# Half of the weight chunks joined on VectorE alone, the other half with two-byte instead of one-byte ScalarE stores, and a Newton step of the norms in three VectorE steps

## The chip, the core and the metric

The kernel runs on one core of one Trainium2 chip. The metric is the device time of one execution in microseconds (us). PE is TensorE (matmuls), DVE is VectorE, ACT is ScalarE, POOL is GpSimd, and SP is the queue that issues most DMAs. Each engine works through its own instructions strictly in their order, and waits on the others by semaphores.

## What is computed

Three layers follow one another on 8 batches of 576 tokens with 512 features: a linear attention, a layer that mixes by two Fourier transforms and a two-matrix network (`moe`), and a gated layer (`moe2`), which the change touches only by its weights.

```python
def _moe_ref(x, w_ch1, w_ch2):                      # x: attention output, (8, 576, 512)
    X = np.fft.fft(np.fft.fft(x, axis=1), axis=2)
    u = x + np.real(X)
    mu = np.mean(u, axis=-1, keepdims=True)
    var = np.mean((u - mu) ** 2, axis=-1, keepdims=True)
    un = (u - mu) / np.sqrt(var + 1e-06)
    return u + np.maximum(un @ w_ch1, 0.0) @ w_ch2   # w_ch1 (512, 2048), w_ch2 (2048, 512)
```

All weight matrices are 64-bit floats in memory.

## The kernel before

**Weights.** The two matrices of `moe` come in as 64-bit numbers and are needed as 32-bit floats. They are cut into 32 chunks of 128 x 512 numbers, two chunks to a pair: 16 pairs, numbered 0 to 15 here. A pair is one buffer of 128 x 1024 numbers, each as a low and a high 32-bit word. `assemble` makes 32-bit floats of it in three passes. `low_parts` issues two: DVE shifts the high words left by three (L168, into `wr`), and ACT takes the top three bits of the low words as a small number and stores it as one byte over the lowest byte of the high word (L169). `high_parts` issues the join one step later: DVE combines both (L171). `squares` (L231, ACT) then sums the squares of the pair, `scales` makes a power of two of the sums of a whole matrix, and `split` writes every chunk as two 16-bit halves (ACT L257, DVE L258). Pairs 0 and 1 have buffers of their own (`words`); from pair 2 on four buffers are taken in turn (`u`, `u`, `raw`, `words`), and the load of pair k+4 (L211, SP) waits for the join of pair k. The same `assemble` serves the weights of the last layer in 40 smaller pieces of 128 x 256, beside the main loop.

**The front.** Before the main loop of matmuls can start, the first batch must have passed attention (L311 on) and the transform (`transform`, L448 on: DVE adds, ACT copies, PE matmuls, in turn), the norm of block 0 must be done (`norm_part`, L599 on), the matrices must be joined and the first chunks split. `beside_first` records these strands into each other: for each step of the attention or transform strand 0.4 steps (`RATE`) of the weight strand `front_z`. The final order on every engine is then set at build time by a scheduler from its own estimates of durations; it is fixed when the kernel runs.

**The main loop** (L1076 on) takes 9 blocks of 512 tokens. Per block PE does 16 times `mm1` (L1093) and `mm2` (L1116); attention, transform and norm of later batches and the last layer's weights run beside it as side work. At a block's end the next block's norm must be done: `halves` (ACT L671, DVE L672) makes its 16-bit parts `unh`, `unl`, and L1134 adds the accumulated result to `u`.

**The norm.** After the mean of squares (PE L632) `norm_part` makes 1/sqrt by ACT (logarithm and exponential, L640 and L641, or L649 and L650), refines it by one Newton step on DVE, and multiplies the deviations `d` by it (L658). For blocks 0 and 1 (`i in SUMS_F32`) that step is four DVE instructions, L643 to L646, on 256 columns at a time; for the other seven blocks one (L648) ahead of the logarithm and three (L653 to L655) behind it, on 512 columns.

Of the kernel before, what the change touches and what calls it, by code (L numbers as in the profile page):

```python
# [10 lines left out]
F16 = mybir.dt.float16  # L11
BF16 = mybir.dt.bfloat16
U32 = mybir.dt.uint32
U8 = mybir.dt.uint8
AF = mybir.ActivationFunctionType
ALU = mybir.AluOpType
AX = mybir.AxisListType
# [11 lines left out]
POOL_K = ()  # L29
BEHIND_X = {(1, 1): 6}  # L30
RATE = 0.4
AHEAD_W = 6
FIRST = 1.0
HOLD = {(2, 0): "c"}

MAX_PE = (0, 1, 2)

POOL_N = ()
SUMS_PE = (0,)
SUMS_F32 = (0, 1)  # L40
# [8 lines left out]
def net(ctx, tc, q, k, v, w1, w2, mu_k, mu_r, w_k, w_v, w_r, ce_d, se_d, cs_d, ss_d, alt_d, id_d, out):  # L49
    nc = tc.nc  # L50
# [65 lines left out]
    wsc = big.tile([128, 8], F32, name="wsc")  # L116
# [44 lines left out]
        nc.sync.dma_start(out=raw.rearrange("p n w -> p (n w)"), in_=src.bitcast(U32)[128 * t:128 * t + 128, 512 * c:512 * c + 512])  # L161
        return raw

    def assemble(raw, x, part=None):

        hi, lo = raw[..., 1], raw[..., 0]
        if part != 1:
            nc.vector.tensor_scalar(out=x, in0=hi, scalar1=3, scalar2=0x3FFFFFFF, op0=ALU.logical_shift_left, op1=ALU.bitwise_and)  # L168
            nc.scalar.activation(out=raw.bitcast(U8)[..., 4], in_=lo, func=AF.Copy, scale=0.9975 * 2.0 ** -29, bias=-0.49)  # L169
        if part != 0:  # L170
            nc.vector.scalar_tensor_tensor(out=x, in0=hi, scalar=0xC0000007, in1=x, op0=ALU.bitwise_and, op1=ALU.bitwise_or)  # L171

    def decode(raw, x):

# [3 lines left out]
    pairs = [(w, c) for w in range(2) for c in range(0, 16, 2)]  # L178
    raws = {}
# [33 lines left out]
    def words_at(w, c):  # L213
        a, b = place[w, c] + 1, place[w, c + 1] + 1
        return wr[:, a:b + 1:b - a]

    def low_parts(k):

        if k < len(pairs):
            assemble(raws[k], words_at(*pairs[k]), 0)  # L220

    def high_parts(k):
        if 0 <= k < len(pairs):
            assemble(raws.pop(k), words_at(*pairs[k]), 1)
# [374 lines left out]
    def norm_part(i, sq, d, rs, c0, n):  # L599
        segs = [(b, s + max(c0 - o, 0), min(o + m, c0 + n) - max(o, c0), max(o, c0)) for b, s, m, o in segments(i) if o < c0 + n and o + m > c0]  # L600
        cs = slice(c0, c0 + n)
        tt = nc.vector.tensor_tensor
# [4 lines left out]
        if not onpe:  # L607
# [3 lines left out]
            pt = mean(i, sq, cs, n)  # L611
        else:
            pt = aside(i == 0, 1)
# [9 lines left out]
        if not onpe:  # L623
# [4 lines left out]
            pt = mean(i, sq, cs, n)  # L628
# [9 lines left out]
        w = sq[:, 1, cs]
        if i in SUMS_F32:
            nc.scalar.activation(out=r, in_=pt[:, 0:n], func=AF.Ln, bias=wsc[:, 7:8])  # L640
            nc.scalar.activation(out=r, in_=r, func=AF.Exp, scale=-0.5)  # L641
            yield 1
            tt(out=v, in0=r, in1=r, op=ALU.mult)  # L643
            nc.vector.scalar_tensor_tensor(out=v, in0=pt[:, 0:n], scalar=1e-6, in1=v, op0=ALU.add, op1=ALU.mult)
            nc.vector.tensor_scalar(out=v, in0=v, scalar1=-0.5, scalar2=1.5, op0=ALU.mult, op1=ALU.add)
            tt(out=r, in0=r, in1=v, op=ALU.mult)  # L646
        else:
            nc.vector.tensor_scalar(out=v, in0=pt[:, 0:n], scalar1=1e-6, scalar2=None, op0=ALU.add)  # L648
            nc.scalar.activation(out=r, in_=v, func=AF.Ln)  # L649
            nc.scalar.activation(out=r, in_=r, func=AF.Exp, scale=-0.5)  # L650
            yield 1

            tt(out=w, in0=r, in1=r, op=ALU.mult)  # L653
            nc.vector.scalar_tensor_tensor(out=w, in0=w, scalar=-0.5, in1=v, op0=ALU.mult, op1=ALU.mult)
            nc.vector.scalar_tensor_tensor(out=r, in0=w, scalar=1.5, in1=r, op0=ALU.add, op1=ALU.mult)  # L655
# [730 lines left out]
```

## Time and profile before

| what | value |
|---|---|
| median of 3 runs (lowest to highest) | 1475.55 us (1475.35 to 1476.8) |
| profiled execution, its own time | 1476.24 us |
| its span in the trace | 1474.5 us |
| busy in the span: PE / DVE / ACT | 1407.6 / 989.5 / 705.6 us |
| mean granted clock of TensorE | 0.976 |

The span is what the trace covers; 1.74 us of the profiled execution's own time lie around it. The profiled execution stands 0.69 us above the median.

### The profile page before, as it was taken

Reading aid. Unit: us, or ns where it says so; the run is one execution under the profiler, and the core shown is the slowest. Engines: PE = TensorE matmul, PEld = TensorE weight load, DVE = VectorE, ACT = ScalarE, POOL = GpSimd, SP = SyncE. Lnnn points to the kernel's source line nnn. Section 1 sums busy time; section 2 is a strip of 40 time slices with the busy share of each in tenths; the row PEclk is TensorE's granted clock in tenths of the full one; section 3 lists DMA queues with packets and bytes.
Section 4 is the critical chain, followed back from the end, with each engine's and each line's share of the span. In section 5 each row is a group of like instructions: output and inputs, shape, how many; then the busy total and the mean of one; then the engine's idle time right before and its main releaser. Section 6 shows DMA issues by size and latency. Waiting matters only on the chain.

```text
span 1474.5 us, 20917 instructions
## 1 busy us (share of the span) xinstructions
PE 1407.6 (95%) x8453; PEld 879.7 (60%) x8453; DVE 989.5 (67%) x1807; ACT 705.6 (48%) x1241; POOL 26.5 (2%) x41
## 2 busy tenths in 40 slices
PE   4559999998999999999999999999999999999998
PEld 3447888996555556556455444445666666666665
DVE  6778676587584765764532476774999788876643
ACT  6895643453342443432321246563766555564421
POOL 0101000000000000000000000000000000000000
PEclk8579999999999999999999999999999999999999
DMA  9731012121110111010010023301011011100001
GB/s 349 251 136 51 1 52 80 51 85 45 51 51 29 51 51 63 17 51 30 0 58 7 32 80 117 118 22 58 29 58 51 8 58 58 50 9 29 30 15 43
DMA packets 38301, 89.47 MB, mean 61 GB/s; under 512 B 5147, under 2 KB 11580, under 8 KB 38204
## 3 DMA queue, kind: packets, MB, share of 16 engines
q1 hardware_dynamic: 37052, 85.30, 16.6%
q0 software_dynamic: 1152, 2.83, 0.6%
q8 instruction: 66, 1.08, 0.3%
q14 instruction: 31, 0.25, 0.1%
HBM read 69.25 MB, written 18.87 MB: 60 GB/s over the span
## 4 chain that ended last, share of the span: by engine, by line
PE 88%; DVE 5%; ACT 4%; issue 1%; DMA 1%; ACTq 0%; DVEq 0%
PE h L1093 24%; PE acc L1116 24%; PE acc L1219 13%; PE h L1154 11%; PE side L1207 6%; PE side L509 2%; PE side L529 2%; PE side L430 2%; PE side L375 1%; ACT u L169 1%; PE side L410 1%; DVE wr L258 1%; DVE wr L171 1%; ACT words L169 1%; DMA kt<-in_k_dram 1%
## 5 line engine op out<-in xcount | busy, mean ns | idle before, releaser
L1093 PE MATMUL h<-unh,wr 128*128 128x512 f16 (+1 forms) x1408 | 381.8, 342 | 3.8 <-ACT unh L671 2.0
L1116 PE MATMUL acc<-hh,wr 128*128 128x512 f16 (+1 forms) x1408 | 370.4, 341 | 0.0
L1093 PEld LDWEIGHTS <-wr 128*128 128x128 f16 x2112 | 203.0, 98 | 169.1 <-issue 7.5
L1116 PEld LDWEIGHTS <-wr 128*128 128x128 f16 x2112 | 201.7, 98 | 160.8 <-issue 3.7
L1093 PE MATMUL h<-unl,wr 128*128 128x512 f16 (+1 forms) x704 | 240.6, 342 | 0.7 <-DVE unl L672 0.7
L1116 PE MATMUL acc<-hl,wr 128*128 128x512 f16 (+1 forms) x704 | 220.0, 341 | 0.0
L1219 PE MATMUL acc<-ring,last 128*128 128x512 f16 x864 | 201.2, 379 | 0.2 <-DVE last L1250 0.2
L1099 DVE SCALAR_TENSOR_TENSOR hl<-h,hh 128x512 f16<-128x512 f32 x144 | 99.0, 687 | 145.8 <-ACT hh L1098 145.2
L1098 ACT ACTIVATE hh<-h 128x512 f16<-128x512 f32 x144 | 85.8, 596 | 180.5 <-PE h L1093 179.8
L1219 PEld LDWEIGHTS <-last 128*128 128x128 f16 x864 | 84.0, 98 | 86.5 <-DVE last L1250 0.7
L1154 PEld LDWEIGHTS <-wkh 128*128 128x128 f16 x1008 | 98.5, 98 | 34.1
L1248 ACT ACTIVATE last<-last,pw 128x512 f32<-128x512 f32 x72 | 51.6, 717 | 106.9 <-DVE last L1247 106.3
L1207 PE MATMUL side<-ring,x 128*128 128x512 f16 x432 | 101.1, 379 | 0.0
L1154 PE MATMUL h<-x,wkh 128*128 128x256 f16 x560 | 95.7, 273 | 0.0
L1169 DVE TENSOR_TENSOR last<-h,last 128x512 f32<-128x512 f32 x90 | 61.8, 687 | 49.9 <-PE h L1154 49.8
L1154 PE MATMUL h<-x,wkl 128*128 128x256 f16 x280 | 76.3, 273 | 0.0
L1154 PE MATMUL h<-last,wkh 128*128 128x256 f16 x448 | 76.1, 273 | 0.0
L1207 PEld LDWEIGHTS <-x 128*128 128x128 f16 x432 | 42.3, 98 | 42.5
L1250 DVE TENSOR_TENSOR last<-last 128x512 f16<-128x512 f32 x72 | 49.5, 687 | 22.1 <-ACT last L1249 21.7
L1154 PE MATMUL h<-last,wkl 128*128 128x256 f16 x224 | 61.1, 273 | 0.0
L883 ACT ACTIVATE aa<-y,ms 128x512 f32<-128x512 f32 x72 | 48.0, 712 | 17.5 <-DVE x L891 12.2
L887 DVE SCALAR_TENSOR_TENSOR aa<-y,ms,aa 128x512 f32<-128x512 f32 x72 | 52.4, 747 | 1.2
(350 smaller groups left out, 2074.2 us busy)
## 6 DMA issues: line engine op xcount, KB each, us to landing
vt<-in_v_dram SPq DMA_DIRECT2D x16, 650.0 KB, 5.0
kt<-in_k_dram SPq DMA_DIRECT2D x16, 576.0 KB, 3.9
qt<-in_q_dram SPq DMA_DIRECT2D x16, 576.0 KB, 3.9
out_dram<-oo SPq DMA_DIRECT2D x36, 256.0 KB, 2.0
y<-yT SPq DMA_DIRECT2D x8, 1026.0 KB, 5.3
u<-in_w_dram SPq DMA_DIRECT2D x16, 512.0 KB, 4.5
words<-in_w_dram SPq DMA_DIRECT2D x10, 512.0 KB, 9.8
raw<-in_w_k_dram SPq DMA_DIRECT2D x16, 256.0 KB, 3.7
```

Source lines behind the costliest of these rows:

```text
L883: nc.scalar.activation(out=a, in_=y[:, t, 0:n], func=AF.Copy, scale=mu[:, w, 1, t:t + 1])
L887: nc.vector.scalar_tensor_tensor(out=a, in0=y[:, t, 1:n + 1], scalar=mu[:, w, 0, t:t + 1], in1=a, op0=ALU.mult, op1=ALU.add)
L1093: mm(out=pt[:, o:o + m], lhsT=a, rhs=c[:, t, o:o + m], start=(t == z == 0), stop=(t == 3 and z == 2))
L1098: ma = nc.scalar.activation(out=hh[:, 0:n], in_=pt[:, 0:n], func=AF.Relu)
L1099: mv = nc.vector.scalar_tensor_tensor(out=hl[:, 0:n], in0=pt[:, 0:n], scalar=0.0, in1=hh[:, 0:n], op0=ALU.max, op1=ALU.subtract)
L1116: mm(out=acc[x][:, o:o + m], lhsT=a, rhs=c[:, o:o + m], start=(f == z == o == 0), stop=(f == NF - 1 and z == 2), skip_group_check=(i < 2))
L1154: mm(out=pt[:, 256 * x:256 * x + 256], lhsT=c[:, u, 128 * x:128 * x + 128], rhs=d[:, u], start=(fresh and x == u == z == 0), stop=(last an ...
L1169: nc.vector.tensor_tensor(out=out, in0=view(pt), in1=addend, op=ALU.add)
L1207: mm(out=pt, lhsT=a[:, v, u, c, o:o + 128], rhs=w[:, t, :], start=(t == y == 0), stop=(t == 3 and y == 2))
L1219: mm(out=acc[x], lhsT=a[:, 128 * x:128 * x + 128], rhs=c[:, f, :], start=(f == z == 0), stop=(f == 7 and z == 2))
L1248: nc.scalar.activation(out=o, in_=o, func=AF.Square, scale=W["pw"][:, 10 + g:11 + g])
L1250: nc.vector.tensor_tensor(out=l2, in0=o, in1=h2, op=ALU.subtract)
```

## The change

`assemble` gets a flag `own`, which is set for the pairs with an even number (0, 2, ... 14; `OWN = 0`). For these the ACT store is left out: a second DVE pass (L170 in the changed file) shifts the low words right by 29 and joins them into `wr`, and the join (L174) then adds only the two top bits of the high words. For the odd pairs, and for the 40 pieces of the last layer, ACT still stores, but two bytes in place of one (L172). In the norm the first of the DVE steps of blocks 2 to 8 goes into the logarithm's bias, which blocks 0 and 1 had already; the factor -0.5 moves from the Newton step into the product with `d`, so that three DVE steps (L644 to L646) stay for every block, and the product (L650) becomes a SCALAR_TENSOR_TENSOR.

```diff
-    def assemble(raw, x, part=None):
+    def assemble(raw, x, part=None, own=False):
         hi, lo = raw[..., 1], raw[..., 0]
+        join = nc.vector.scalar_tensor_tensor
         if part != 1:
             nc.vector.tensor_scalar(out=x, in0=hi, scalar1=3, scalar2=0x3FFFFFFF, op0=ALU.logical_shift_left, op1=ALU.bitwise_and)
-            nc.scalar.activation(out=raw.bitcast(U8)[..., 4], in_=lo, func=AF.Copy, scale=0.9975 * 2.0 ** -29, bias=-0.49)
+            if own:
+                join(out=x, in0=lo, scalar=29, in1=x, op0=ALU.logical_shift_right, op1=ALU.bitwise_or)
+            else:
+                nc.scalar.activation(out=raw.bitcast(U16)[..., 2], in_=lo, func=AF.Copy, scale=0.9975 * 2.0 ** -29, bias=-0.49)
         if part != 0:
-            nc.vector.scalar_tensor_tensor(out=x, in0=hi, scalar=0xC0000007, in1=x, op0=ALU.bitwise_and, op1=ALU.bitwise_or)
+            join(out=x, in0=hi, scalar=0xC0000000 if own else 0xC0000007, in1=x, op0=ALU.bitwise_and, op1=ALU.bitwise_or)
...
-            assemble(raws[k], words_at(*pairs[k]), 0)
+            assemble(raws[k], words_at(*pairs[k]), 0, k % 2 == OWN)
...
-            tt(out=v, in0=r, in1=r, op=ALU.mult)
-            nc.vector.scalar_tensor_tensor(out=v, in0=pt[:, 0:n], scalar=1e-6, in1=v, op0=ALU.add, op1=ALU.mult)
-            nc.vector.tensor_scalar(out=v, in0=v, scalar1=-0.5, scalar2=1.5, op0=ALU.mult, op1=ALU.add)
-            tt(out=r, in0=r, in1=v, op=ALU.mult)
-        else:
-            nc.vector.tensor_scalar(out=v, in0=pt[:, 0:n], scalar1=1e-6, scalar2=None, op0=ALU.add)
...
+        tt(out=v, in0=r, in1=r, op=ALU.mult)
+        nc.vector.scalar_tensor_tensor(out=v, in0=pt[:, 0:n], scalar=1e-6, in1=v, op0=ALU.add, op1=ALU.mult)
+        nc.vector.scalar_tensor_tensor(out=r, in0=v, scalar=-3.0, in1=r, op0=ALU.add, op1=ALU.mult)
         yield 0
         for x in range(2):
-            (nc.gpsimd.tensor_tensor if i in POOL_N else tt)(out=d[:, 2 * x:2 * x + 2, cs], in0=d[:, 2 * x:2 * x + 2, cs], in1=r[:, None, :].to_broadcast([128, 2, n]), op=ALU.mult)
+            dx = d[:, 2 * x:2 * x + 2, cs]
+            nc.vector.scalar_tensor_tensor(out=dx, in0=dx, scalar=-0.5, in1=r[:, None, :].to_broadcast([128, 2, n]), op0=ALU.mult, op1=ALU.mult)
```

The changed file is eight lines shorter, so that line numbers behind the norm are eight lower in it, and those in attention and transform three higher. The scheduler's order changes in the whole front. Three places follow.

On ACT, in the front, from the store of pair 4 to the attention of the first batch's second half, before (`qT`, `kt`, `qt`: attention; `wr,amax`: squares):

```order
L169 ACTIVATE raw<-raw 128x1024
L403 ACTIVATE qT<-side_311 128x4x128
L403 ACTIVATE qT<-acc_317 128x4x128
L403 ACTIVATE qT<-acc_329 128x2x64
L231 ACTIVATE wr,amax<-wr 128x1024
L364 ACTIVATE kt<-kt 128x1152
L169 ACTIVATE words<-words 128x1024
L231 ACTIVATE wr,amax<-wr 128x1024 x2
L357 ACTIVATE qt<-qt 128x1152
L169 ACTIVATE u<-u 128x1024
```

The same stretch of ACT with the change:

```order
L234 ACTIVATE wr,amax<-wr 128x1024
L406 ACTIVATE qT<-side_311 128x4x128
L406 ACTIVATE qT<-acc_317 128x4x128
L367 ACTIVATE kt<-kt 128x1152
L406 ACTIVATE qT<-acc_329 128x2x64
L234 ACTIVATE wr,amax<-wr 128x1024
L172 ACTIVATE words<-words 128x1024
L234 ACTIVATE wr,amax<-wr 128x1024 x2
L360 ACTIVATE qt<-qt 128x1152
L388 ACTIVATE kvbd_99<-acc_291,rk 64x64 x4
```

The stores of pairs 4 (`raw`) and 6 (`u`) are gone; that of pair 5 (`words`) stays, and is followed by the same squares and `qt`.

On DVE, a little later in the front, around the joins of pairs 6 and 7 (both `u`), before (`st`, `qt`, `kvbd`: attention; `eo`: transform):

```order
L366 TENSOR_REDUCE st<-qt 128x18
L387 COPY kvbd_99<-kvbd_99 64x2
L171 SCALAR_TENSOR_TENSOR wr<-u,wr 128x2x512
L367 TENSOR_SCALAR st<-st 128x18
L168 TENSOR_SCALAR wr<-u 128x2x512
L368 RECIPROCAL st<-st 128x18
L370 TENSOR_TENSOR qt<-qt,st 128x1152
L464 TENSOR_TENSOR eo<-u 128x288 x2
L171 SCALAR_TENSOR_TENSOR wr<-u,wr 128x2x512
L464 TENSOR_TENSOR eo<-u 128x288 x2
```

The same stretch of DVE with the change:

```order
L170 SCALAR_TENSOR_TENSOR wr<-u,wr 128x2x512
L370 TENSOR_SCALAR st<-st 128x18
L174 SCALAR_TENSOR_TENSOR wr<-u,wr 128x2x512
L371 RECIPROCAL st<-st 128x18
L373 TENSOR_TENSOR qt<-qt,st 128x1152
L467 TENSOR_TENSOR eo<-u 128x288 x2
L168 TENSOR_SCALAR wr<-u 128x2x512
L467 TENSOR_TENSOR eo<-u 128x288 x2
L472 TENSOR_TENSOR x_97<-eo,x_97 1x289
L478 TENSOR_TENSOR eo<-eo 128x289
L174 SCALAR_TENSOR_TENSOR wr<-u,wr 128x2x512
```

Pair 6 now has two DVE passes there (L170, L174) and no ACT store to wait for. The first pass of pair 7 (L168) has moved behind the second half of the attention, so that four instructions of the transform stand between it and its join, where before the end of the attention (L368, L370) stood there too.

On DVE, at the end of the front, from the norm of block 0 to the first `split`, before (`sq`, `rs`, `d`: norm; `m`: attention of the next batch; `wsc<-amax`: scales):

```order
L643 TENSOR_TENSOR rs<-rs 128x256
L336 TENSOR_TENSOR m<-m,kt 64x128
L644 SCALAR_TENSOR_TENSOR rs<-side_581,rs 128x256
L645 TENSOR_SCALAR rs<-rs 128x256
L171 SCALAR_TENSOR_TENSOR wr<-u,wr 128x1024
L646 TENSOR_TENSOR rs<-rs 128x256
L643 TENSOR_TENSOR rs<-rs 128x256
L658 TENSOR_TENSOR d<-d,rs 128x2x256 x2
L644 SCALAR_TENSOR_TENSOR rs<-acc_588,rs 128x256
L240 TENSOR_REDUCE wsc<-amax 128x1
L258 SCALAR_TENSOR_TENSOR wr<-wr,wsc 128x512
```

The same stretch of DVE with the change:

```order
L609 TENSOR_TENSOR sq<-u 128x2x64
L336 TENSOR_TENSOR m<-m,kt 128x256
L339 TENSOR_TENSOR m<-m,kt 64x128 x2
L644 TENSOR_TENSOR rs<-rs 128x256
L645 SCALAR_TENSOR_TENSOR rs<-side_581,rs 128x256
L644 TENSOR_TENSOR rs<-rs 128x256
L646 SCALAR_TENSOR_TENSOR rs<-rs 128x256
L243 TENSOR_REDUCE wsc<-amax 128x1
L645 SCALAR_TENSOR_TENSOR rs<-acc_588,rs 128x256
L650 SCALAR_TENSOR_TENSOR d<-d,rs 128x2x256
L261 SCALAR_TENSOR_TENSOR wr<-wr,wsc 128x512
```

The join of the last pair, 15, has left this stretch: it now stands ahead of it, right behind the subtraction that makes `d` (L621, before L618). One of the two products with `d` comes behind the first split.

## Rows read from the trace of the kernel before

**Rows 1.** Windows: busy time of each engine in stretches, granted clock, DMA

```profile
18.00:109.00 91.00, 47.47 (x203) 39.11 (x201) 66.56 (x117) 81.34 (x117) 4.97 (x8) 0.69 0.62 230
...
160.00:480.00 320.00, 315.63 (x2292) 239.15 (x2290) 211.67 (x370) 132.20 (x254) 7.05 (x8) 0.99 0.15 51
480.00:1022.00 542.00, 542.00 (x2708) 279.60 (x2707) 319.98 (x603) 216.96 (x436) 5.50 (x9) 1.00 0.15 47
1022.00:1474.50 452.50, 448.19 (x2856) 276.51 (x2854) 335.65 (x621) 236.37 (x368) 3.24 (x7) 1.00 0.12 40
```

The columns are: stretch, its length, busy us (and count) of PE, PEld, DVE, ACT and POOL, granted clock, DMA share, GB/s.

**Rows 2.** Waits of DVE from 18 to 109 us: total us, times, longest

```profile
DVE wr L171 <- ACT words L169: 8.5, 5, 3.3
DVE wr L171 <- ACT u L169: 5.5, 5, 1.8
DVE sq L606 <- PE acc L632: 3.2, 1, 3.2
DVE wr L171 <- ACT raw L169: 2.2, 3, 1.3
DVE wr L171 <- ACT seh L137: 2.0, 1, 2.0
DVE wsc L343 <- PE acc L341: 1.3, 1, 1.3
DVE eo L464 <- ACT u L431: 0.5, 1, 0.5
```

**Rows 3.** Line L169, the one-byte stores: ns minimum/median/maximum, first and last start

```profile
L169 ACT ACTIVATE raw<-raw x43: 759/831/2481, 37.8 to 985.3; 128x256 uint8<-128x256 uint32 x40, 128x1024 uint8<-128x1024 uint32 x3
L169 ACT ACTIVATE u<-u x8: 2459/2469/2620, 29.1 to 103.1; 128x1024 uint8<-128x1024 uint32 x8
L169 ACT ACTIVATE words<-words x5: 2457/2471/2533, 18.8 to 88.5; 128x1024 uint8<-128x1024 uint32 x5
```

**Rows 4.** Groups by form, 0 to 160 us: busy us, mean ns, idle before

```profile
L231 ACT ACTIVATE wr<-wr 128x1024 bf16<-128x1024 f32 x16 | 16.9, 1059 | 2.4 <-DVE wr L171 2.2
...
L171 DVE SCALAR_TENSOR_TENSOR wr<-u,wr 128x1024 uint32<-128x1024 uint32 x8 | 9.8, 1223 | 7.5 <-ACT u L169 5.5 <-ACT seh L137 2.0
...
L403 ACT ACTIVATE qT<-side 128x512 f32<-128x512 f32 x6 | 6.9, 1145 | 0.0
...
L168 DVE TENSOR_SCALAR wr<-u 128x1024 uint32<-128x1024 uint32 x8 | 5.4, 678 | 0.0
```

**Rows 5.** Timeline of DVE in the front: start, us, instruction, idle before it

```profile
88.63 0.75 DVE L552 TENSOR_TENSOR u<-u,sd 128x574 f32<-128x574 f32 x1
...
93.11 2.35 DVE L618 TENSOR_TENSOR d<-u,acc 128x1024 f32<-128x1024 f32 x2
...
102.84 0.29 DVE L606 TENSOR_TENSOR sq<-u 128x128 f32<-128x128 f32 x1 [3.23 <-PE acc L632]
...
104.93 0.29 DVE L645 TENSOR_SCALAR rs<-rs 128x256 f32<-128x256 f32 x1
...
109.06 0.75 DVE L258 SCALAR_TENSOR_TENSOR wr<-wr,wsc 128x512 f16<-128x512 f32 x1
```

**Rows 6.** Timeline of PE, the sums of squares of the norm of block 0

```profile
96.88 3.78 PE L632 MATMUL side<-sq,onesr 128*128 128x256 f32 x8 [1.85 <-ACT sq L620]
100.45 2.28 PE L632 MATMUL acc<-sq,onesr 128*128 128x256 f32 x8
```

**Rows 7.** Line L648, the first step of the later norms: ns minimum/median/maximum

```profile
L648 DVE TENSOR_SCALAR rs<-side x7: 692/692/692, 336.5 to 866.8; 128x512 f32<-128x512 f32 x7
```

**Rows 8.** Timeline of PE, the rows with idle time from 345 to 350 us

```profile
346.12 0.59 PE L1093 MATMUL h<-unh,wr 128*128 128x512 f16 x2 [1.96 <-ACT unh L671]
348.84 0.61 PE L430 MATMUL side<-qT,bdh 128*128 128x288 f32 x1 [2.12 <-DVE qTl L405]
```

**Rows 9.** Waits of the SP queue in the whole span: total us, times, longest

```profile
SPq L211 <- DVE wr L171: 40.2, 8, 9.5
```

**Rows 10.** DMA queues from 0 to 110 us

```profile
DMA packets 7680, 27.15 MB, mean 247 GB/s; under 512 B 859, under 2 KB 1020, under 8 KB 7676
```

More of the change, by code (lines that the diff above doesn't have):

```diff
@@ L13 @@
 U32 = mybir.dt.uint32
-U8 = mybir.dt.uint8
+U16 = mybir.dt.uint16
 AF = mybir.ActivationFunctionType
@@ L31 @@
 RATE = 0.4
+OWN = 0
 AHEAD_W = 6
@@ L36 @@
 MAX_PE = (0, 1, 2)
-POOL_N = ()
 SUMS_PE = (0,)
-SUMS_F32 = (0, 1)
 JT = (((0, 128), (128, 128), (225, 64)), ((0, 128), (128, 128), (256, 32)))
@@ L219, in low_parts @@
         if k < len(pairs):
-            assemble(raws[k], words_at(*pairs[k]), 0)
+            assemble(raws[k], words_at(*pairs[k]), 0, k % 2 == OWN)
     def high_parts(k):
         if 0 <= k < len(pairs):
-            assemble(raws.pop(k), words_at(*pairs[k]), 1)
+            assemble(raws.pop(k), words_at(*pairs[k]), 1, k % 2 == OWN)
             if k + 4 >= AHEAD_W:
@@ L637, in norm_part @@
         v, r = rs[:, 0, cs], rs[:, 1, cs]
[L638 to L642, printed above, removed]
-            tt(out=v, in0=r, in1=r, op=ALU.mult)
-            nc.vector.scalar_tensor_tensor(out=v, in0=pt[:, 0:n], scalar=1e-6, in1=v, op0=ALU.add, op1=ALU.mult)
-            nc.vector.tensor_scalar(out=v, in0=v, scalar1=-0.5, scalar2=1.5, op0=ALU.mult, op1=ALU.add)
-            tt(out=r, in0=r, in1=v, op=ALU.mult)
-        else:
-            nc.vector.tensor_scalar(out=v, in0=pt[:, 0:n], scalar1=1e-6, scalar2=None, op0=ALU.add)
[L649 to L655, printed above, removed]
+        nc.scalar.activation(out=r, in_=pt[:, 0:n], func=AF.Ln, bias=wsc[:, 7:8])
+        nc.scalar.activation(out=r, in_=r, func=AF.Exp, scale=-0.5)
+        yield 1
+        tt(out=v, in0=r, in1=r, op=ALU.mult)
+        nc.vector.scalar_tensor_tensor(out=v, in0=pt[:, 0:n], scalar=1e-6, in1=v, op0=ALU.add, op1=ALU.mult)
+        nc.vector.scalar_tensor_tensor(out=r, in0=v, scalar=-3.0, in1=r, op0=ALU.add, op1=ALU.mult)
         yield 0
         for x in range(2):
-            (nc.gpsimd.tensor_tensor if i in POOL_N else tt)(out=d[:, 2 * x:2 * x + 2, cs], in0=d[:, 2 * x:2 * x + 2, cs], in1=r[:, None, :].to_broadcast([128, 2, n]), op=ALU.mult)
+            dx = d[:, 2 * x:2 * x + 2, cs]
+            nc.vector.scalar_tensor_tensor(out=dx, in0=dx, scalar=-0.5, in1=r[:, None, :].to_broadcast([128, 2, n]), op0=ALU.mult, op1=ALU.mult)
             yield 0
```

## The prediction

> **What bounds the kernel now.** I read the windows first. From 160 us to the end PE is busy for all but 4.4 + 0 + 4.3 us of 1314 [rows 1]: there the kernel is PE's own work, which the change leaves alone, and what DVE or ACT save costs and gains nothing. From 18 to 109 us it is different. PE is busy 47.5 of 91 us at a granted clock of 0.69, ACT 81.3 us, DVE 66.6 us [rows 1]. ACT sets the pace of this front, and DVE must be watched, since the change hands it work.
>
> The waits of DVE in these 91 us show how ACT's load reaches the end. DVE is idle 91.0 - 66.6 = 24.4 us, and 8.5 + 5.5 + 2.2 = 16.2 us of it end with a byte store of L169; 2.0 more end with a tiny ACT row (L137) that stands behind such a store, and 1.3 with a PE transpose that waits for an ACT copy behind the first store [rows 2]. The stores are long: 2.47 us for 128 x 1024, where a squares pass over as many elements takes 1.06 us [rows 3, 4]. Sixteen of them (8 + 5 + 3) are 39.5 us, half of ACT's load.
>
> The timeline of DVE has the end of the front: the mean of block 0 is taken off at 93.1 to 95.5, DVE then waits 3.2 us for PE's sums of squares, and the first split starts at 109.06 [rows 5]. So I ask when the first split starts in the changed kernel; what follows it is the same list of DVE work, and everything behind moves with it.
>
> **Part by part.**
>
> *Eight ACT stores removed.* This takes 8 x 2.47 = 19.8 us from ACT. No price follows from that directly, since ACT then has some 62 of 91 us to do and stops being the limit; the gain is what DVE no longer waits.
>
> *Eight DVE passes added.* The added pass (shift and or, two inputs, 128 x 1024 words) does not occur in the trace. The nearest row is the join, the same instruction on the same operands with other operators: 1.22 us [rows 4]. Bounds: the one-input first pass, 0.68 us [rows 4], and the join. I take the join. Rows that do not depend on each other overlap by about 0.08 us in the timeline, so 8 x 1.15 = 9.2 us. At 0.68 us each the sum would be 3.8 us better.
>
> *Eight ACT stores of two bytes.* No ACT row writes two-byte elements eight bytes apart. Bounds: 1.06 us, as for squares, and 2.47 us as now [rows 3, 4]. Between them lies the copy into `qT`, which writes four-byte elements 16 bytes apart: 1.145 us for 512, twice the element count of which would take at most twice as long, 2.3 us (estimate) [rows 4]. I take 2.47 us: the byte store is the nearest row in operands and step, and only the width differs. [...]
>
> *What is late next.* With the order of the changed program I laid DVE's and ACT's rows from 18 us on end to end, with the durations of the trace. Between a remaining store's first pass and its join DVE mostly has 2.5 to 5.5 us of other work, so that 2.47 us are covered. Three are not: pair 5, whose store stands behind two `qT` copies, an exponential and a squares pass on ACT (1.9 us of wait), pair 7, between whose first pass and join only about 1.7 us of transform rows stand (0.9 us), and pair 9 (0.3 us): 3.1 us. Two waits on PE come up because DVE is there earlier: 0.5 us at the second transform and 0.9 us at the mean of block 0. The wait for the sums of squares stays: PE needs 3.78 + 2.1 us behind `d` [rows 6], DVE has 3.3 us to do beside it (last join, `kt`, `m`), so 2.6 us remain of 3.2.
>
> *The norm.* On the way to the first split one `L645` of 0.29 us goes [rows 5], and one product with `d` (0.64 us) now comes behind the split. For blocks 2 to 8 DVE saves 0.69 us each [rows 7], 4.8 us in all, under a busy PE: nothing. Only at the turn to block 2 does PE wait, 1.96 and 2.12 us [rows 8]. There the chain loses L648, but three of the updates of `u` (some 2.6 us) now stand ahead of the product with `d` where one stood, while the second wait's releaser comes about 1 us earlier: I take 0, with 1.5 us either way. The product as SCALAR_TENSOR_TENSOR has the rate of the join (1.22 us for 1024) against 1.2 us per product in the row of L618 [rows 4, 5]: nothing. If PE were not the cover there, all of it would be worth under 5 us.
>
> *Loads.* The load of pair k+4 waits for the join of pair k, eight times, 40 us in all [rows 9]. The queue runs ahead with the joins. All bytes up to 110 us are 27.15 MB at a mean of 247 GB/s [rows 10]; the laid-out order needs them about 8 us sooner, 7% more, and no DVE row in that stretch waited for a landing. I take 0.
>
> *Sum.* First split after 18 us: 91.0 + 9.2 (passes) - 19.5 (16.2 + 2.0 + 1.3) - 1.0 (of the 24.4 - 22.7 us that the first six rows of waits leave, mostly handovers from ACT copies that stood behind stores, as the 0.5 us at L464 [rows 2]) + 3.1 + 1.4 - 0.6 - 0.3 - 0.6 = 82.7 us, so at 100.8 instead of 109.06: 8.2 us. Laid end to end the order gives 101.0, which agrees; I take 8.1. The profiled execution would come to 1476.24 - 8.1 = 1468.1, and the median, which stands 0.69 us lower, to **1467.5 us**.
>
> **The rivals.**
>
> *More is gained.* If a two-byte store takes 1.06 us, the waits for pairs 7 and 9 go and that of pair 5 shrinks to 0.5 us, 2.6 us in all; ACT copies of the transform come a further 1 us sooner. That is 11.7 us: 1463.9. The bound on this side is a DVE that waits for nothing before the first split: 24.4 - 9.2 + 0.2 = 15.4 us, 1460.2. For it speaks that nothing but width seems special about these stores; against it the copy into `qT`, where four-byte elements are slow too. Chance 0.22.
>
> *Less is gained, because the attention and transform strand sets the end.* Attention, transform and norm hand over some nine times between PE, ACT and DVE, with PE at clock 0.69. I found waits at two of these; with 0.5 us more at each of nine, 4.5 us, the gain is 3.6: 1472. For it speaks that laid end to end this strand's last addition to `u` ends only 2.5 us sooner (86.9 against 89.4 [rows 5]), since the new passes stand between its rows; the rest of the gain comes from weights that are done earlier. Chance 0.20.
>
> *Slower: the strand was the limit all along.* Then byte stores cost DVE only time in which the strand would have kept it waiting anyway, and the passes are put in its way: + 9.2 - 2.0 - 1.3 - 0.2 = + 5.7 us, 1481.2. It decides when more than 24.4 - 9.2 = 15.2 us of DVE idle remain up to the first split. Against it: L403, L431 and L516 of the strand, too, stood behind stores on an ACT that was busy 81 of 91 us. Chance 0.08.
>
> **How the numbers follow.** The forecast, a gain of 5.5 to 9.5 us, has chance 0.50, and by itself a range of 1466 to 1470. The range for 8 in 10 leaves out the upper half of the first rival and the slower end of the others: 1462 to 1473. A measurement here can tell 0.2%, 2.95 us, from no change. Faster by more: 0.50 + 0.22 + two fifths of 0.20, = 0.80. Slower: 0.07. Same: 0.13.
>
> **What would show it.** Right: in the changed trace 16 first passes, 8 added passes near 1.22 us, 8 stores; DVE busy about 75 us up to the first split, which starts near 101 us; ACT clearly below DVE there; waits on stores of 3 us instead of 16; the stretch from the first split to the end as long as before, to 1.5 us. A store of 1.1 us would speak for the first rival, DVE waits on PE or on ACT copies of 10 us or more for the second and third. The forecast is wrong altogether if PE's list behind 160 us gets new gaps, of which the order shows no sign except at the turn to block 2.

## The result and the profile after

The changed kernel takes 1462.28 us (median of 4 runs, 1461.51 to 1462.93) against 1476.17 us before, measured on the same chip: ratio 0.9905, 95% interval 0.9888 to 0.9922. The gain is 13.9 us, the forecast said 8.1. The profiled execution of the changed kernel took 1462.37 us, its span is 1460.6 us.

The page's totals:

```profile
PE 1406.6 (96%) x8453; PEld 879.3 (60%) x8453; DVE 991.7 (68%) x1804; ACT 689.9 (47%) x1233; POOL 27.3 (2%) x41
```

PE's and DVE's totals are those of before to 2.2 us; ACT has 15.7 us less. The windows say where that mattered (columns as in [rows 1]); the first one ends with the first split, at 95.49 us instead of 109.06 [rows 5]:

```profile
18.06:95.49 77.43, 46.76 (x205) 38.36 (x204) 73.22 (x123) 63.02 (x108) 5.05 (x8) 0.76 0.71 270
...
466.00:1008.00 542.00, 542.00 (x2699) 278.46 (x2698) 316.15 (x596) 218.59 (x436) 5.50 (x9) 1.00 0.15 47
1008.00:1460.60 452.60, 448.32 (x2857) 276.60 (x2855) 335.68 (x622) 236.38 (x368) 3.26 (x7) 1.00 0.12 40
```

The front is 13.6 us shorter. From the first split to the end it is 1365.1 us, against 1365.4 before, and the two late windows are those of before [rows 1]. In the front DVE is idle 77.43 - 73.22 = 4.2 us where it was idle 24.4. Its waits there, in total us, times and longest, are these few:

```profile
DVE wr L174 <- ACT words L172: 1.5, 2, 1.0
DVE sd L545 <- PE side L536: 1.1, 1, 1.1
DVE wr L174 <- ACT u L172: 0.8, 1, 0.8
DVE d L621 <- PE acc L619: 0.2, 1, 0.2
```

16.2 us of waits on stores have become 2.3. The wait for the sums of squares, 3.2 us before, of which 2.6 were to stay, is not in the list. The groups by form have the disputed prices (busy us, mean ns, idle before):

```profile
L170 DVE SCALAR_TENSOR_TENSOR wr<-u,wr 128x1024 uint32<-128x1024 uint32 x4 | 4.9, 1214 | 0.0
...
L172 ACT ACTIVATE words<-words 128x1024 uint16<-128x1024 uint32 x4 | 10.0, 2506 | 2.6 <-DVE wr L168 2.6
L172 ACT ACTIVATE u<-u 128x1024 uint16<-128x1024 uint32 x4 | 10.0, 2491 | 0.3 <-DVE wr L168 0.3
```

The added pass costs 1.21 us, as the join does, and two bytes cost what one byte cost, 2.5 us [rows 3]. The sums of squares on PE (timeline):

```profile
87.78 1.98 PE L635 MATMUL side<-sq,onesr 128*128 128x256 f32 x8
89.59 1.89 PE L635 MATMUL acc<-sq,onesr 128*128 128x256 f32 x8
```

The same sixteen rows took 3.78 + 2.28 us before [rows 6]. The granted clock was 0.50, half the full clock, between 95 and 100 us then and is 1.00 between 85 and 95 now. From the mean of block 0 on PE had idled 5.24, 2.00 and 1.85 us (the last one is in [rows 6]); now it idles 3.99, 0.98 and 0.80. PE's rows before:

```profile
85.39 3.78 PE L616 MATMUL acc<-u,onesr 128*128 128x256 f32 x8 [5.24 <-DVE u L545]
...
94.08 0.94 PE L347 MATMUL side<-m,one 128*128 128x256 f32 x2 [2.00 <-ACT m L346]
```

And with the change:

```profile
79.64 3.40 PE L619 MATMUL acc<-u,onesr 128*128 128x256 f32 x8 [3.99 <-DVE u L548]
...
84.45 1.99 PE L619 MATMUL acc<-u,onesr 128*128 128x256 f32 x8 [0.98 <-DVE u L554]
87.24 0.70 PE L350 MATMUL side<-m,one 128*128 128x256 f32 x2 [0.80 <-ACT m L349]
```

What PE waited for just ahead of the sums, the squares of `d` on ACT (L620), had itself stood behind a store. Before, the store of pair 14 ran from 93.94 us on, and the squares started at 96.15, 3.0 us after the first row of `d` on DVE (93.11 [rows 5]):

```profile
93.94 2.46 ACT L169 ACTIVATE u<-u 128x1024 uint8<-128x1024 uint32 x1
96.15 0.67 ACT L620 ACTIVATE sq<-d 128x512 f32<-128x512 f32 x1
```

Pair 14 is one of those that DVE now joins alone. The squares (L623) start 1.5 us after the first row of `d` (85.62):

```profile
87.10 0.61 ACT L623 ACTIVATE sq<-d 128x512 f32<-128x512 f32 x1
```

The turn to block 2 is still there, with 3.2 us of idle PE against 4.4 (1.96 + 2.12 [rows 8] and 0.29 behind them):

```profile
332.82 1.01 PE L1085 MATMUL h<-unh,wr 128*128 128x512 f16 x2 [2.67 <-ACT unh L663]
334.38 0.58 PE L433 MATMUL side<-qT,bdh 128*128 128x288 f32 x1 [0.54 <-DVE qTl L408]
```

### The profile page after: what moved, and what is told of

It reads as the page before. It is cut to its first block, busy times and chain, and to the rows that moved or that the text cites. A ratio compares the mean times of both kernels' runs of the same rounds, so it can differ in the third digit from the quotient of the medians.

```text
span 1460.6 us, 20917 instructions
## 1 busy us (share of the span) xinstructions
PE 1406.6 (96%) x8453; PEld 879.3 (60%) x8453; DVE 991.7 (68%) x1804; ACT 689.9 (47%) x1233; POOL 27.3 (2%) x41
## 4 chain that ended last, share of the span: by engine, by line
PE 89%; DVE 6%; ACT 2%; issue 1%; DMA 1%; POOL 0%; DVEq 0%; SPq 0%; POOLq 0%
PE h L1085 24%; PE acc L1108 24%; PE acc L1211 13%; PE h L1146 11%; PE side L1199 6%; PE side L532 2%; PE side L512 2%; PE side L433 2%; PE side L378 1%; PE side L413 1%; DVE wr L261 1%; DMA kt<-in_k_dram 1%; DVE wr L174 0%; DVE wr L168 0%; DVE eo L467 0%
## 5 line engine op out<-in xcount | busy, mean ns | idle before, releaser
L1085 PE MATMUL h<-unh,wr 128*128 128x512 f16 (+1 forms) x1408 | 380.8, 342 | 6.1 <-ACT unh L663 3.9
L1108 PE MATMUL acc<-hh,wr 128*128 128x512 f16 (+1 forms) x1408 | 369.8, 341 | 0.0
L1085 PEld LDWEIGHTS <-wr 128*128 128x128 f16 x2112 | 202.1, 98 | 170.6 <-issue 8.1
L1108 PEld LDWEIGHTS <-wr 128*128 128x128 f16 x2112 | 202.2, 98 | 160.5 <-issue 3.0
L1085 PE MATMUL h<-unl,wr 128*128 128x512 f16 (+1 forms) x704 | 240.0, 341 | 0.0
L1108 PE MATMUL acc<-hl,wr 128*128 128x512 f16 (+1 forms) x704 | 219.4, 340 | 0.0
```

What stands on the lines that cost most here:

```text
L1085: mm(out=pt[:, o:o + m], lhsT=a, rhs=c[:, t, o:o + m], start=(t == z == 0), stop=(t == 3 and z == 2))
L1108: mm(out=acc[x][:, o:o + m], lhsT=a, rhs=c[:, o:o + m], start=(f == z == o == 0), stop=(f == NF - 1 and z == 2), skip_group_check=(i < 2))
```

## The experiments

Theory: the gain is the eight stores taken from ACT, and what DVE does and waits for up to the first split sets the time. Rivals: two-byte stores are cheaper, the norm brings the gain, or the strand of attention and transform is the limit.

**The three parts, each alone.** `assemble` with `own` for the even pairs, but one-byte stores and the old norm (the join and the calls are as in the change):

```diff
-            nc.scalar.activation(out=raw.bitcast(U8)[..., 4], in_=lo, ...)
+            if own:
+                nc.vector.scalar_tensor_tensor(out=x, in0=lo, scalar=29, in1=x, op0=ALU.logical_shift_right, op1=ALU.bitwise_or)
+            else:
+                nc.scalar.activation(out=raw.bitcast(U8)[..., 4], in_=lo, ...)
```

> The kernel before with one part of the change: the even pairs are joined on VectorE alone; the stores of the odd pairs stay one byte wide and the norm stays as it was. Theory A (the gain is VectorE's waits on eight long ScalarE stores, less eight passes of 1.14 us): nearly the whole gain, 12 to 14 us, so 1462 to 1464 us, first split near 96 to 97 us. Theory B (the three parts share the gain, or the scheduler's new order of the norm's rows gives the clock of the sums of squares): 5 to 9 us, so 1467 to 1471 us.

Measured: 1462.71 us, ratio 0.9912 (0.9899 to 0.9926). The window up to the first split, which is nearly that of the whole change:

```profile
18.06:95.75 77.69, 45.63 (x205) 37.84 (x204) 73.78 (x126) 63.06 (x108) 4.70 (x8) 0.76 0.72 270
```

So this part is the gain. The new order of the front, which the scheduler makes for it, comes along with it and was not tried apart. The stores of two bytes alone:

```diff
-            nc.scalar.activation(out=raw.bitcast(U8)[..., 4], in_=lo, ...)
+            nc.scalar.activation(out=raw.bitcast(U16)[..., 2], in_=lo, ...)
```

> The kernel before with two-byte in place of one-byte stores for all 16 pairs and the 40 pieces of the last layer, nothing else; the order of VectorE's instructions is that of before. Theory A (a store costs the same 2.5 us at either width): 1476 us, unchanged within 0.1%, L169 at 2.45 to 2.52 us. Theory B (width counts as soon as nothing else differs): stores of 1.1 us and 8 us or more gained.

Measured: 1476.69 us, ratio 1.000 (0.9991 to 1.0009). The line's durations (ns minimum/median/maximum) are those of [rows 3]; this part does nothing:

```profile
L169 ACT ACTIVATE u<-u x8: 2462/2466/2599, 29.0 to 103.6; 128x1024 uint16<-128x1024 uint32 x8
```

The norm alone, that is the changed kernel with one-byte stores and no pair `own`:

```diff
-            assemble(raws[k], words_at(*pairs[k]), 0, k % 2 == OWN)
+            assemble(raws[k], words_at(*pairs[k]), 0, False)
```

> The kernel before with the three-step Newton of the norms alone; every pair has its one-byte ScalarE store. Theory A (under a busy TensorE it is worth 0.3 us at the end of the front and 0 to 1.5 us at the turn to block 2): 1475 us, 0 to 2 us gained. Theory B (it shortens the norm's chain by more, through the order or the clock): 3 us or more gained.

Measured: 1474.32 us, ratio 0.9991 (0.9983 to 1.0). The first split starts at 109.14 us, as before; the turn to block 2 waits 3.7 us where it waited 4.4:

```profile
344.54 0.59 PE L1085 MATMUL h<-unh,wr 128*128 128x512 f16 x2 [2.73 <-ACT unh L663]
346.09 0.58 PE L433 MATMUL side<-qT,bdh 128*128 128x288 f32 x1 [0.96 <-DVE qTl L408]
```

**All sixteen pairs on DVE.**

```diff
-            assemble(raws[k], words_at(*pairs[k]), 0, k % 2 == OWN)
+            assemble(raws[k], words_at(*pairs[k]), 0, True)
```

> The changed kernel with all 16 pairs joined on VectorE alone, so that ScalarE stores nothing in the front. Theory A (VectorE now sets the pace: 73.2 us of its 77.4 us up to the first split are busy): eight more passes of 1.14 us less the 2.3 us that it still waits for stores, so 6 to 8 us slower than the changed kernel, 1468 to 1470 us, first split near 102 us. Theory B (ScalarE or the attention and transform strand still sets it): within 2 us of the changed kernel.

Measured: 1469.64 us, ratio 0.9954 (0.9942 to 0.9966), 7.4 us slower than the change.

```profile
18.07:103.98 85.91, 47.37 (x206) 38.36 (x206) 82.32 (x132) 46.11 (x100) 5.18 (x8) 0.72 0.66 244
```

Eight passes more make DVE 9.1 us busier and the front 8.5 us longer, while ACT loses 16.9 us: ACT is no limit any more at this end. The first split is 2 us later than Theory A has it; the time is in its range.

**Six own pairs in place of eight.**

```diff
-            assemble(raws[k], words_at(*pairs[k]), 0, k % 2 == OWN)
+            assemble(raws[k], words_at(*pairs[k]), 0, k % 3 == OWN)
```

> The changed kernel with pairs 0, 3, 6, 9, 12 and 15 joined on DVE alone (6 of 16 in place of 8); ten pairs keep ACT's store in place of eight. Theory A (with the change the front is bound by DVE's own work, 73.2 us busy of 77.4, and what is taken from DVE comes back in part): DVE's busy time falls by 2 x 1.2 = 2.4 us, its waits for stores grow by 1 to 4 us (two more stores of 2.5 us on ACT), first split at 94 to 97.5 us, time 1461 to 1464.5. Theory B (the waits for ACT's stores are what set the front, each store left is one wait): every store added costs as a store of before did, 13.6 us by 8 or 1.7 us each, time 1465.5 to 1466.5.

Measured: 1462.04 us, ratio 0.9906 (0.9891 to 0.9922). The time is Theory A's, and the mechanism is not: the first split starts at 104.89 us, 9.4 later than with the change. DVE's waits up to there (total us, times, longest):

```profile
DVE wr L174 <- ACT words L172: 4.8, 2, 2.5
DVE sd L545 <- PE side L536: 3.7, 1, 3.7
DVE wr L174 <- ACT seh L136: 2.6, 1, 2.6
DVE wr L174 <- ACT u L172: 2.4, 3, 1.3
DVE wr L174 <- ACT raw L172: 1.6, 1, 1.6
```

Pairs 1 and 2, 4 and 5, and so on now store one behind the other, and 11.4 us of waits end with a store or the row behind it. What the front lost came back later, 9.6 us of it. The window from 325 to 350 us, of the change first and of this kernel second:

```profile
325.00:350.00 25.00, 21.79 (x130) 15.53 (x129) 19.76 (x36) 10.19 (x22) 0.00 (x0) 0.86 0.24 71
```

```profile
325.00:350.00 25.00, 25.00 (x180) 18.32 (x178) 22.39 (x37) 10.55 (x18) 1.48 (x1) 1.00 0.20 67
```

There is no wait at the turn to block 2 in this kernel, and no fall of the clock after it.

**The clock in the front.** To the kernel before, eight products with unused results are added on PE ahead of the sums of squares:

```diff
             mv = tt(out=d[:, :, o:o + m], in0=U[b][:, :, s:s + m], in1=pt[...], op=ALU.subtract)
+        if i == 0 and c0 == 0:
+            warm(8, d[:, 0, 0:128])
```

> The kernel before with eight added matmuls of 128x128 (results unused) on PE between the ones of m (L347) and the sums of squares of block 0, made as soon as the first deviations are there. Theory A (the sums of squares cost DVE 3.2 us because PE had been idle for 5.2, 2.0 and 1.9 us and was granted half its clock in that stretch; the change took 2 us of its extra gain there, where its idler DVE let PE come back to the full clock): the first eight products of that group fall from 3.78 to about 2.0 us and the second from 2.28 to about 1.9, DVE's wait of 3.23 us for them falls below 2, the first split comes 1 to 2.2 us earlier, and the time is 1474 to 1475.2 us. Theory B (the join waits for ACT's store behind it in any case, so that a faster PE gives nothing): the group may be faster, but the wait for the store grows by as much, and the time stays at 1476.2 within 0.5 us.

Measured: 1474.33 us, ratio 0.9988 (0.9979 to 0.9996).

```profile
94.13 1.95 PE L442 MATMUL h<-d,onesr 128*128 128x128 f32 x16
96.41 1.99 PE L634 MATMUL side<-sq,onesr 128*128 128x256 f32 x8 [0.33 <-ACT sq L622]
98.24 1.89 PE L634 MATMUL acc<-sq,onesr 128*128 128x256 f32 x8
```

```profile
100.24 0.29 DVE L606 TENSOR_TENSOR sq<-u 128x128 f32<-128x128 f32 x1 [0.64 <-PE acc L634]
```

The rows behind the added work run at 1.00 of the clock, DVE's wait falls from 3.23 to 0.64 us, and the first split comes 2.1 us earlier, at 106.96. The added work kept the clock up here rather than raising it: the row ahead of it (L347) already took 0.70 us, where it took 0.94 before. In the profile of the run with two-byte stores alone, which has no added work and the PE order of before, L347 took 0.70 us as well, but PE then idled, and the sums that follow took 3.78 + 3.11 us:

```profile
96.54 3.78 PE L632 MATMUL side<-sq,onesr 128*128 128x256 f32 x8 [2.10 <-ACT sq L620]
```

So Theory A holds.

**The order at the turn.** In the changed kernel six of the eight updates of `u` (L1126) stand on DVE ahead of, or between, the last step of the norm and the products with `d`. Here all eight wait for the 16-bit parts of block 2:

```diff
+        if i == 2:
+            mark("halves", mv)
...
-                nc.vector.scalar_tensor_tensor(out=y, in0=acc[x][:, o:o + m], ...)
+                with behind("halves" if i == 1 else None):
+                    nc.vector.scalar_tensor_tensor(out=y, in0=acc[x][:, o:o + m], ...)
```

> The changed kernel with the eight updates of u at the end of block 1 held on DVE until the 16-bit parts of block 2 are made; six of them, 2.48 us, stood ahead of the products with d, for whose parts PE waits 2.67 us. Theory A (what is left of the wait at that turn is the order on DVE): the products with d start some 2.4 us earlier, the wait on the first part falls below 0.7 us, and the time is 1458.8 to 1460.8 us. Theory B (another wait takes its place, for the tail of attention or for the accumulators that the updates now free later): the sum of PE's waits between 325 and 345 us stays at 2.5 to 4 us, and the time is 1461.5 to 1463.5.

Measured: 1459.97 us, ratio 0.9891 (0.9878 to 0.9905), 2.3 us less than the change, with the first split 1.1 us later (96.57). PE's rows with idle time at the turn:

```profile
331.83 0.59 PE L1087 MATMUL h<-unh,wr 128*128 128x512 f16 x2 [0.56 <-ACT unh L663]
338.98 1.05 PE L1110 MATMUL acc<-hh,wr 128*128 128x512 f16 x4 [0.25 <-DVE u L1129]
341.23 0.39 PE L512 MATMUL side<-ceh,eh 128*128 128x258 f32 x1 [1.21 <-DVE yl L522]
```

3.2 us of idle have become 2.0: most of Theory A, with a part of what Theory B named, a wait for the updates and one for the transform behind them. The granted clock does not fall either; from 325 to 350 us it is 1.00, where it was 0.86:

```profile
325.00:350.00 25.00, 22.90 (x141) 14.60 (x140) 21.49 (x35) 10.40 (x19) 0.06 (x1) 1.00 0.20 66
```

**The price of the stores, alone.** ACT copies 128 x 1024 values in twelve forms:

```diff
+    writes = {"u8_step8": st(d8, 8), "u16_step8": st(d16, 4), "f32_step8": st(d32, 2), "u32_step8": st(du, 2),
+              "u8": st(d8, 1), "u16": st(d16, 1), "f32": st(d32, 1)}
...
+        nc.scalar.activation(out=writes[w], in_=reads[r], func=AF.Copy, scale=0.9975 * 2.0 ** -29, bias=-0.49)
```

> Nothing of the reference is computed: ACT alone copies 128 x 1024 values, four times in each of twelve forms, with one, two or four bytes stored and 32-bit whole numbers or floats read, at a step of 8 bytes or one behind the other. In the kernels the store of one or two bytes from whole numbers, both at a step of 8 bytes, took 2.46 to 2.54 us, and squares of floats one behind the other 1.06. Theory A (the step of the store makes the price): every form that stores at a step of 8 bytes takes 2.4 to 2.6 us, four bytes from floats too, and every form that stores one behind the other 1.0 to 1.3. Theory B (the reading of whole numbers makes it): every form that reads whole numbers takes 2.4 to 2.6 us wherever it stores, and the forms that read floats 1.0 to 1.3. Theory C (the width below four bytes makes it): one and two bytes take 2.4 to 2.6 us at any step, four bytes 1.0 to 1.3.

One row each of the timeline; the view doesn't show steps. In order they are: four bytes at a step of 8 bytes, one byte and two bytes at that step, one and two bytes without gaps (all five from whole numbers at a step), and four bytes without gaps from whole numbers without gaps; then, from floats without gaps, one byte at the step, four bytes at the step, and one byte without gaps:

```profile
12.02 1.15 ACT L75 ACTIVATE fd<-src 128x1024 f32<-128x1024 uint32 x1
13.07 2.44 ACT L75 ACTIVATE dst<-src 128x1024 uint8<-128x1024 uint32 x1
19.55 2.44 ACT L75 ACTIVATE dst<-src 128x1024 uint16<-128x1024 uint32 x1
32.51 1.10 ACT L75 ACTIVATE dst<-src 128x1024 uint8<-128x1024 uint32 x1
40.31 1.11 ACT L75 ACTIVATE dst<-src 128x1024 uint16<-128x1024 uint32 x1
41.30 1.06 ACT L75 ACTIVATE fd<-src 128x1024 f32<-128x1024 uint32 x1
...
48.23 2.50 ACT L75 ACTIVATE dst<-fs 128x1024 uint8<-128x1024 f32 x1
53.69 1.21 ACT L75 ACTIVATE fd<-fs 128x1024 f32<-128x1024 f32 x1
...
61.27 1.08 ACT L75 ACTIVATE dst<-fs 128x1024 uint8<-128x1024 f32 x1
```

All three theories fall. Neither the step alone (1.15, 1.21 us) nor the narrow type alone (1.10, 1.11) costs anything to speak of, nor does the reading; only narrow elements stored at a step of 8 bytes cost 2.4 to 2.5 us. Other steps were not tried here, and the result must not be read as leave for every gap of four-byte stores: the copy into `qT`, which stores four bytes at a step of 16 bytes, takes 1.145 us for 512 values [rows 4], where squares of `d` store 512 without gaps in 0.61 to 0.68 us.

**Four-byte stores in the kernel.** This suggests a third way to join a pair, for weights below 2 in size, here with no `own` pair:

```diff
+        if part is not None and not own:
+            if part == 0:
+                nc.scalar.activation(out=lo, in_=lo, func=AF.Copy, scale=0.9975 * 2.0 ** -29, bias=-0.49)
+            else:
+                join(out=x, in0=hi, scalar=3, in1=lo, op0=ALU.logical_shift_left, op1=ALU.bitwise_or)
+                join(out=x, in0=hi, scalar=0x3FFFFFFF, in1=x, op0=ALU.bitwise_or, op1=ALU.bitwise_and)
+            return
```

> The changed kernel with all sixteen pairs joined in a third way: ACT stores the top three bits of the low word as four bytes in the place of the low word, one store to every pair, and DVE makes two passes of SCALAR_TENSOR_TENSOR behind it (shift left and join; then the two top bits, for weights below 2). The copies alone showed 1.15 us for four bytes at a step of 8 bytes against 2.44 for one or two. Theory A (that price holds in the kernel, and the front is bound by DVE's work): DVE's passes are 16 x 2.45 = 39.2 us against 8 x 3.1 + 8 x 1.9 = 40.0 of the changed kernel, ACT's stores 16 x 1.15 = 18.4 against 19.8; first split at 93.5 to 97.5 us, time 1460 to 1463.5. Theory B (beside the loads of the front four bytes cost as much as two): sixteen stores of 2.4 us, ACT 38 us, waits for stores as in the kernel before, time 1470 to 1477.

Measured: 1452.6 us, ratio 0.9835 (0.9822 to 0.9849), the fastest version but for a tie (next run) and 9.7 us less than the change. The store's durations, and the windows of the front and of the turn:

```profile
L169 ACT ACTIVATE u<-u x8: 1132/1146/1191, 25.3 to 80.7; 128x1024 uint32<-128x1024 uint32 x8
```

```profile
18.06:95.29 77.23, 45.17 (x208) 37.50 (x206) 72.93 (x117) 60.93 (x116) 4.60 (x8) 0.77 0.73 271
...
325.00:350.00 25.00, 25.00 (x149) 15.56 (x148) 14.53 (x26) 7.24 (x15) 0.00 (x0) 1.00 0.18 64
```

The price holds in the kernel, and the first split (95.29 us) is where Theory A has it. The time is 7 us below Theory A's range, and the gain lies behind the front, as in the kernel with six own pairs: no wait at the turn. Together with the held updates:

> The same four-byte stores for all sixteen pairs, and the eight updates of u at the end of block 1 held behind the 16-bit parts of block 2. Theory A (the two are separate, front and turn): what the holding gave the changed kernel, 2.3 us, comes off the time of the four-byte stores alone, less what its turn no longer waits there. Theory B (whichever of the two makes the loop reach block 2 sooner, the side work of block 2 is not ready before about 331 us of the span, and a gain in the front is spent there): the time stays at 1459 to 1461.5, as that of the changed kernel with the holding.

Measured: 1452.01 us, ratio 0.9834 (0.9821 to 0.9848), the same time: the updates of `u` follow the 16-bit parts by themselves in the four-byte kernel, so nothing was left to hold. Theory B's bound of 1459 was wrong.

**What decides the turn.** On PE the kernels come in three fixed orders. I counted the products of the main loop, L1085 and L1108 in the changed kernel, that stand ahead of the last sums of squares of block 2's norm (768 of each end block 1):

| kernel | ahead of the sums | PE idle at the turn |
|---|---|---|
| before, own pairs alone, two bytes alone, added products | 768 and 698 | 4.3 to 4.4 us |
| change, norm alone, all pairs own, held updates | 768 and 718 | 2.0 to 3.7 us |
| six own pairs, four-byte stores (all three runs with them), pair 0 by store | 744 and 677 | none |

To part this from the front and from the stores, pair 0 of the change, too, is given a two-byte store, which makes the third order:

```diff
-            assemble(raws[k], words_at(*pairs[k]), 0, k % 2 == OWN)
+            assemble(raws[k], words_at(*pairs[k]), 0, k % 2 == 0 and k != 0)
```

> The changed kernel with pair 0, the first of all, joined with a two-byte store like the odd pairs; seven pairs are joined on DVE alone. On PE the order at the end of block 1 comes out otherwise: the sums of squares of block 2's norm, which stand behind 768 and 718 products of the two kinds of the main loop in the changed kernel, stand behind 744 and 677, as in the kernels with every third pair and with four-byte stores, the two that had no wait at that turn. Theory A (the place of these sums on PE decides the turn, whatever the front does): PE busy for all of 325 to 350 us at the full clock, 7 us less from the first update of u to the end of the two-matrix network, time 1453.5 to 1457.5 with a front that ends 1 us earlier to 3 us later. Theory B (the four-byte stores, or a front that ends later, made the side work early against the loop; the order on PE only follows): waits of 2.5 to 4 us remain at the turn and the time is 1461 to 1464.

Measured: 1462.56 us, ratio 0.9905 (0.989 to 0.992). The turn is as Theory A has it, the front is not: its first split starts at 104.28 us, with 7.0 us of waits on stores, and with the wait for the sums of squares back. A store stands on ACT ahead of the squares of `d` again (from 91.20 us on), PE idles 1.57 us, and the first eight sums take 3.78 us:

```profile
100.82 0.29 DVE L609 TENSOR_TENSOR sq<-u 128x128 f32<-128x128 f32 x1 [3.49 <-PE acc L635]
```

```profile
325.00:350.00 25.00, 25.00 (x182) 18.49 (x180) 22.99 (x40) 10.31 (x18) 1.48 (x1) 1.00 0.20 67
```

The total is Theory B's by a cancellation, as with six own pairs. The last run joins the even pairs on DVE and gives the odd ones four-byte stores (the edit above, with `own` kept):

> The changed kernel with four-byte stores and two DVE passes behind them for the odd pairs, the even pairs on DVE alone as in the change. Against the changed kernel ACT has 8 x 1.3 = 10.6 us less in the front and DVE 8 x 0.54 = 4.3 us more. The sums of block 2's norm stand early on PE here too. Theory A (with the change DVE's work alone bounds the front, and ACT's is worth nothing more): DVE's waits fall from 4.2 to about 2.5 us, the first split comes 2 to 4 us later than in the changed kernel, at 97.5 to 99.5, and with the turn's 7 us taken off the time is 1456.5 to 1459. Theory B (ACT's stores still bound the front): the first split comes earlier, at 91 to 95 us, and the time is 1448 to 1454.

Measured: 1457.55 us, ratio 0.9871 (0.9855 to 0.9888), first split at 99.61 us: Theory A.

```profile
18.06:99.61 81.55, 46.90 (x208) 37.90 (x207) 78.09 (x125) 53.97 (x109) 4.59 (x8) 0.74 0.70 258
```

Against the change ACT has 9.0 us less and DVE 4.9 more, and the front is 4.1 us longer.

The milestones of these runs, in us from the start of the span (first split; first update of `u` at the end of block 0; start of the last product of the two-matrix network):

| kernel | split | block 0 done | network done | from block 0 |
|---|---|---|---|---|
| before | 109.06 | 226.99 | 1021.79 | 794.8 |
| change | 95.49 | 213.77 | 1007.92 | 794.2 |
| all pairs own | 103.98 | 221.89 | 1015.40 | 793.5 |
| change, updates held | 96.57 | 214.88 | 1005.52 | 790.6 |
| six own pairs | 104.89 | 220.61 | 1007.74 | 787.1 |
| pair 0 by store | 104.28 | 220.94 | 1008.36 | 787.4 |
| own and four bytes | 99.61 | 215.42 | 1002.61 | 787.2 |
| four bytes | 95.29 | 211.17 | 998.15 | 787.0 |

The kernels with the sums early on PE take 6.7 to 7.2 us less from block 0 on than the change, whether their front is long or short, and a long front alone (all pairs own, first split at 103.98 us) takes off 0.6. Most of the 7 us are the 3.2 us of idle and, as an estimate, 3.5 us of a granted clock of 0.86 over 25 us. That the place of the sums on PE is the cause is not shown. In the kernels with the sums early all eight updates of `u` also stand behind the 16-bit parts on DVE (in the four-byte kernel the parts start at 323.70 us and the updates at 326.31). The run with the held updates has that order on DVE with the sums late on PE, and it takes off 3.5 us from block 0 on. The other half was seen only with the sums early; no run moved the sums on PE and nothing else.

The four-byte kernel's gain over the change, 9.7 us, is these 7.2, 0.2 in the front and 2.4 between the first split and the end of block 0, where PE idles 1.5 us in place of 4.4. The last part was not tried by itself.

## Why the prediction came out as it did

**The mechanism was right, its size too small.** The own pairs alone gave all of the gain but what the norm adds, and the time from the first split to the end did not change, as forecast. The size was missed: 13.9 us lie outside the forecast gain of 5.5 to 9.5, and the time is only 0.3 us inside the range for 8 in 10. That it is inside is partly luck, since the fast side of that range was drawn for cheaper stores, which did not come. The sum made the front 82.7 us, and it is 77.4. The missing 5.3 us are two things: DVE's idle time is 4.2 us instead of 7.8, and its busy time rose by 6.7 us instead of 8.3.

**The wait for the sums of squares, -0.6 in the sum, should have been -3.2.** That is 2.6 us, half of the miss and the term that was mis-sized most: "PE needs 3.78 + 2.1 us behind `d`" took PE's durations as fixed. They were those of a granted clock of 0.50 to 0.88, after long idle times of PE, and shorter idle times ahead took them to 1.98 + 1.89. One of these idle times was itself the work of a removed store, that of pair 14 ahead of the squares of `d`. The added products showed the same on the kernel before, with DVE's wait down by 2.6 us, at 2.1 us of the first split; and the run with pair 0 by store shows the reverse, a store ahead of the squares and the wait of 3.5 us back.

**The eight passes, +9.2, and the two norm rows, -0.9.** The price was right, 1.21 us. Summed over the groups of DVE up to the first split (that split left out), the durations rise by 82.2 - 73.8 = 8.4 us, as priced, but busy time, which counts overlapping time once, by 6.7. Rows that no longer wait start while the row ahead still ends; I had counted that for the added passes alone. That is 1.6 us.

**The residual waits, +3.1 and +1.4.** They came at the three stores named, pairs 5, 7 and 9, as 1.0, 0.8 and 0.4 us, 0.8 less in all. The two waits on PE are 1.1 + 0.2. No other handover grew, and no row of DVE waited for a load, which the prediction took at 0.

**Two-byte stores at 2.47 us.** Right; alone they change nothing. The Trainium skill (ScalarE: Activation LUTs, What ACT_TABLE_LOAD costs) has 186 ns + 0.833 ns per element for an ACTIVATE with immediate scale and bias, with a rate that it states for fp32 and bf16; that is 1.04 us as an estimate here. The runs agree for stores without gaps and for four-byte elements at a step of 8 bytes (1.06 to 1.21 us), and for one or two bytes at that step the measured 2.44 to 2.62 us decide.

**The norm and the turn at 0, 1.5 us either way.** From block 0 on the change is 0.6 us shorter than before. Alone on the kernel before, the norm gave some 2 us by the medians, at the edge of what can be told. Front and turn were right to be summed apart here, since the order on PE at the turn differed by 20 products only; I didn't see that the turn held 7 us. So the prediction's sentence that behind 160 us nothing is to be gained from DVE or ACT does not hold: the held updates, another order of DVE's rows at that turn, made the kernel 2.3 us faster than the change.

**The rivals.** The first, more gained, has the size and not the mechanism: the stores are not cheap, and at 13.6 us the gain is above its 11.7 and below its bound of 15.4 (which gives the norm's rows 0.2 us where the sum gives them 0.9; with 0.9 it is 16.1). The second and the third fall: the last addition to `u` ended at 85.1 us, not at 86.9, and the strand set no pace.

**DVE or ACT.** The prediction let the limit pass from ACT to DVE. That is half of it. Towards more DVE work (all pairs own, own and four bytes) the front grows by 0.85 to 0.93 us for each us of DVE's busy time, with ACT ever idler. Towards one or two stores more it grows by 9 us: 11.4 us (two stores more) and 7.0 us (one more) of waits end with stores, 3.7 and 3.5 us with PE, and the granted clock in the front is 0.73 and 0.70 in place of 0.76. The change sits where both meet; why one more store costs so much was only read from the waits.

## What to carry to other kernels

Before pricing a removed wait, look at what the waiting had cost elsewhere: PE's rows behind long idle times ran at half the clock, and shorter waits gave that back. Where a scheduler fixes the order, count what stands ahead of the critical rows in each version: an edit in the front moved the sums of a norm by some 65 products, and the updates of `u` on DVE with them, at a turn 220 us later, with 7 us less in those kernels, half of what the change itself gained; and a total that does not move can hide two moves of 8 to 10 us. Price a store with gaps from a row of the same width and step: here narrow results were slow at a step of 8 bytes, and four-byte ones were not.

## What was not expected of the hardware

- ScalarE stores of 128 x 1024: 1.06 to 1.21 us for four bytes without gaps or at a step of 8 bytes, and 1.07 to 1.12 us for one or two bytes without gaps, but 2.44 to 2.50 us for one or two bytes at a step of 8 bytes.
- TensorE's same sixteen rows took 6.1 us at a granted clock of 0.50 to 0.88, behind 5.2, 2.0 and 1.9 us of idle time, and 3.9 us at 1.00, behind 4.0, 1.0 and 0.8 us of idle time, or behind eight added products.
